# A new written-out order for all engines in sliding-window attention followed by an ELU feed-forward layer

## The chip, the cores and the metric

The kernel runs on one core of a Trainium2 chip. The metric is device time in microseconds (us); lower is better. A core has five engines that run side by side, each strictly in the order of its own instruction stream: TensorE (PE, matrix products), VectorE (DVE), ScalarE (ACT), GpSimd (POOL) and SyncE (SP, which here only issues DMA transfers). They wait for each other on semaphores. Matrix products land in PSUM, a small memory of eight banks, and have to be taken from there by DVE or ACT. TensorE's clock is granted by a throttle, and the profile shows which share of it was granted.

## The reference

There are 8 batches, 8 heads, 576 positions and a head size of 64. Attention is limited to a window of 32 positions to each side; its output, 4608 tokens of width 512, goes through two matrix products with an ELU between them.

```python
def _attn_ref(q, k, v):
    scores = (1.0 / np.sqrt(D)) * np.matmul(q, k.transpose(0, 1, 3, 2))
    mask = np.abs(pos[:, None] - pos[None, :]) <= 32
    scores = np.where(mask, scores, -1000000000.0)
    attn = np.exp(scores - np.max(scores, axis=-1, keepdims=True))
    attn = attn / (np.sum(attn, axis=-1, keepdims=True) + 1e-09)
    return np.matmul(attn, v)

def _moe_ref(x, w_in, w_out):          # x: 4608 x 512, w_in: 512 x 2048
    h = x @ w_in
    g = np.where(h > 0.0, h, np.exp(np.minimum(h, 0.0)) - 1.0)
    return g @ w_out                   # w_out: 2048 x 512

x = attn_out.transpose(0, 2, 1, 3).reshape(B * S, H * D)
```

## The kernel before

**Tiling.** The work unit is 64 query positions of one batch with all heads; there are 9 units in a batch and 72 in all. Two neighbouring units mostly form a group (`G`, line 409): groups 0 to 4 are batch 0, 5 to 8 batch 1. A group goes through these steps, and the name in brackets is the step's name in the plan: scores of all heads by 8 or 16 small products (QK, line 431), the exponential on ACT (SM, 444), the window mask on DVE (MK, 459), product with V in two halves of four heads (AV, 472), where a column of ones beside V gives the row sums, division by them on DVE (RN, 495 and 497), and a transpose of the result into `xt` (X). The transpose is a product with the identity on PE (513) and a copy for groups 0 to 8, and a transposing DMA on SP (509) from group 9 on.

Units are then gathered into token tiles of 2, 2, 2, 3, 4, 3 and then 8 units (`sizes`, line 597). For a tile the first product with w_in is done in pieces of up to 512 columns (H, line 537) into the three PSUM banks `psH`; ACT takes the exponential (EX, 546), ACT or DVE forms the clamped part (FF, 558 or 560), and DVE takes the maximum into `g_sb` (GG, 566 or 569), which frees the bank. `g_sb` holds 1024 tokens. Each chunk of 128 tokens is then multiplied with w_out in four parts of four products (Y, line 584), one for each quarter of w_out, all into one bank; ACT copies the result out (YC, 590) and issues the store (OUT, 594).

**Loads.** K, Q and V come as 32-bit blocks of 128 positions from SP (L, line 271; the blocks at the end are shorter). V blocks are cast into `vw` (CV, from line 345). From batch 2 on a K block and a Q block lie side by side in one buffer `sp`, are cast together on POOL (C2, line 311) and transposed by one DMA (XB, 324). For batch 0 the first half of the positions is loaded, cast (C), transposed on PE (T, 337) and copied (E). The second half of batch 0's K and Q and all of batch 1's come as 16-bit data by four and two DMAs from POOL (LR, line 363 on, issued at 383), are transposed on PE in small pieces (TR, 393) and copied (TTR). The weights too come from POOL, as four quarters each: `WI(c)` (655) and `WO(c)` (660). Quarter c of w_in serves the columns fo from 4c to 4c + 3; quarter c of w_out serves part c of each Y. All loads from POOL stand behind one wait (WAIT, 291) for batch 0's first Q block.

**What sets the order.** Nothing in the kernel is scheduled by a compiler. The class `Plan` (line 21) holds every step with its engine, an assumed duration, a rank and the steps that it depends on; it plays through a small model of the engines and of the DMA queues, and whenever an engine is free it takes the ready step with the lowest rank. The order that comes out is the order in which the instructions are issued; the chip then keeps each engine to it. `SHIFT` (618) moves single ranks, `ENG` (611) gives single steps to another engine, `DLAT` (33) is the assumed time from a transfer's end to its use, `RING` (643) how many transfers SP keeps outstanding, `LATE` an extra delay for two loads. The ranks of the loads of batch 0 start from the place in `FIRST` (721), those of POOL's queue from the place in `LINE` (723). Steps that hold a buffer (`psH`, `st`, `sp`, `cb`) are only taken when one is free in the model.

While the model has PE idle in the first 30 us (`WARM`), PE gets filler: products of the identity with itself into an unused corner of a PSUM bank (line 484). Their number comes from the idle time in the model:

```python
if start[n] < self.WARM:
    self.fill(max(0, int((start[n] - pe - 0.15) / 0.11)))
```

The dependency of a Y part on its quarter of w_out is written with an offset for chunk 0, so part 0 of chunk 0 names quarter 2, and its parts 1 to 3 name quarter 3; the product itself reads quarter `part`:

```python
deps.append(("WO", min(NWC - 1, part * YQ * NWC // NFO + 2 * (c == 0))))
```

Of the kernel before, what the change touches and what calls it, by code (L numbers as in the profile page):

```python
# [20 lines left out]
class Plan:  # L21
# [11 lines left out]
    DLAT = 1.9  # L33
# [22 lines left out]
    def run(self):  # L56
# [22 lines left out]
        def push(t, kind, x):  # L79
            heapq.heappush(events, (t, kind, next(seq), x))  # L80
# [23 lines left out]
        while len(order) < len(ops) or events or any(rings.values()):  # L104
# [4 lines left out]
            if nxt is not None and (te is None or now + nxt <= te):  # L109
                now += nxt  # L110
                for q in rings.values():
                    if q:
                        q[0][1] -= nxt / per
                        if q[0][1] <= 1e-9:
                            h = q.pop(0)
                            for a, k in self.acq.get(h[0], ()):
                                if a == "ring":
                                    held[a] += k
                                    for e in free:
                                        push(now, 1, e)  # L120
                            push(now + self.DLAT + self.late[h[0]], 0, h[0])
                continue
# [44 lines left out]
        for n in order:  # L167
            if ops[n][0] == "PE":
                if start[n] < self.WARM:
                    self.fill(max(0, int((start[n] - pe - 0.15) / 0.11)))  # L170
                pe = start[n] + ops[n][1]
            ops[n][4]()
# [3 lines left out]
def kernel(  # L176
# [423 lines left out]
    for t, n in enumerate(sizes):  # L600
# [11 lines left out]
        ("TT", 0, "k", 1): "DVE", ("CV", 0, 0, 1): "POOL", ("CV", 0, 2, 1): "DVE", ("CV", 0,  # L612
        2, 2): "ACT", ("C", 0, "q", 2): "POOL", ("TTR", 0, "k", 0): "ACT", ("TTR", 0, "k",
        1): "DVE", ("TTR", 0, "q", 1): "DVE", ("TTR", 1, "k", 1): "DVE", ("TTR", 1, "k", 2):
        "ACT", ("TTR", 1, "k", 3): "DVE", ("X", 5): "DVE", ("X", 6): "DVE", ("FF", 0, 8):
        "ACT", ("FF", 2, 8): "ACT", ("FF", 4, 0): "ACT", ("FF", 4, 2): "DVE", ("FF", 4, 8):
        "ACT", ("FF", 4, 14): "DVE", ("FF", 5, 8): "DVE", ("FF", 5, 14): "DVE"}
    SHIFT = {
        ("zvw", 2): 926, ("WI", 0): 54, ("WI", 1): 60, ("WI", 2): 47, ("WO", 0): 49, ("WO",
        1): 57, ("LR", 1, "k", 0): 107, ("LR", 1, "q", 0): 110, ("WO", 3): 61, ("L", 0, "k",  # L620
        0): 100, ("L", 0, "k", 1): 103, ("L", 0, "q", 0): 97.6, ("L", 0, "v", 0): 97, ("L",
        0, "v", 1): 30, ("L", 0, "k", 2): 100, ("L", 0, "q", 1): 35, ("L", 0, "v", 2): 85,
        ("L", 0, "q", 2): 99, ("C", 0, "q", 2): -1931, ("L", 0, "v", 3): 91, ("L", 1, "v",
        1): 219, ("GT", 2): 128, ("TT", 2, 0): 15, ("TT", 2, 2): 7, ("TT", 2, 4): 5, ("TT",
        3, 0): -10, ("TT", 3, 3): 9, ("TT", 3, 4): 2, ("TT", 4, 1): -9, ("TT", 4, 2): -5,
        ("TT", 4, 3): -31, ("TT", 4, 4): -40, ("TT", 5, 1): -102, ("TR", 0, "k", 1): -129,
        ("TR", 0, "q", 0): -179, ("TR", 1, "k", 0): -44, ("TR", 1, "q", 0): -16, ("TR", 1,
        "q", 1): -15, ("TR", 1, "q", 2): -40, ("TR", 1, "q", 3): -44, ("MK", 2): -1957,
        ("AV", 2, 1): -133, ("QK", 4): -168, ("RN", 4, 1): -2043, ("XT", 5): 64, ("QK", 6):
        -27, ("AV", 6, 0): 33, ("RN", 7, 0): -2117, ("XT", 7): 41, ("SM", 8): -2119, ("AV",  # L630
        8, 1): 42, ("AV", 9, 0): 98, ("X", 9): 19, ("RN", 10, 1): 85, ("X", 10): 16, ("QK",
        11): 58, ("X", 11): 14, ("X", 15): 8, ("X", 17): 2, ("QK", 19): -111, ("X", 19):
        -66, ("AV", 20, 1): -109, ("SM", 21): 43, ("AV", 21, 1): 21, ("RN", 21, 1): 21,
        ("H", 0, 0): -86, ("H", 0, 4): -191, ("GG", 0, 8): -2059, ("H", 1, 0): -59, ("H", 1,
        8): -181, ("H", 1, 12): -174, ("GG", 1, 12): -2063, ("H", 2, 4): -205, ("H", 2, 8):
        -187, ("H", 2, 12): -82, ("H", 3, 0): -75, ("H", 3, 4): -62, ("H", 3, 8): -217,
        ("FF", 3, 10): -2123, ("H", 3, 12): -29, ("H", 3, 14): 43, ("H", 4, 0): 26, ("H", 4,
        2): 45, ("H", 4, 6): -162, ("H", 4, 8): 44, ("H", 4, 10): -154, ("H", 4, 12): 69,
        ("H", 4, 14): -153, ("H", 5, 0): 49, ("H", 5, 2): 72, ("H", 5, 4): 96, ("GG", 5, 4):
        88, ("H", 5, 6): 73, ("H", 5, 8): 18, ("H", 5, 12): 91, ("H", 5, 14): 39, ("Y", 0,  # L640
        0): -95, ("Y", 0, 3): -64, ("Y", 1, 0): -66, ("Y", 1, 3): -58, ("Y", 2, 1): -45,
        ("Y", 2, 2): -41, ("Y", 2, 3): 36, ("Y", 4, 2): 72, ("Y", 11, 0): -126}
    RING, XBT = 2.2, 1.3
    LATE = {("L", 0, "v", 3): 1.0, ("L", 0, "v", 4): 1.0}
# [105 lines left out]
    for b in range(B):  # L750
        blocks = sorted(((group_of(b, nm, j), "kqv".index(nm), nm, j)
                         for nm in "kqv" for j in range(NTB)))
        for _, _, nm, j in blocks:
# [5 lines left out]
            if b:  # L759
                deps = [("GT", min(b, 2))]  # L760
                if deps[0] not in P.ops:
# [4 lines left out]
            pk = PK[nm][j] if b or nm == "v" or j < 2 else 16  # L766
            P.op(n, "SP", 0.62, rl, deps,
                 lambda b=b, nm=nm, j=j: L(b, nm, j, nc.sync),
                 dma=("S", pk, 16 if b else 15), late=LATE.get(n, 0.0),
                 acq=[("st", 1) if nm == "v" else ("sp", 0.5), ("ring", 1)])  # L770
# [31 lines left out]
            if nm == "k":  # L802
                continue
            r = min(r, prank(group_of(b, "k", j)))
            P.op(("C", b, j), "POOL", 1.25, r - CC, [("L", b, "k", j), n],
                 lambda b=b, j=j: C2(b, j, nc.gpsimd),
                 acq=("cb", 1), rel=("sp", 1))
            war = [("QK", qk(last(b - NKB)))] if b >= NKB else []
            P.op(("TT", b, j), "SP", XBT, r - XX, [("C", b, j)] + war,
                 lambda b=b, j=j: XB(b, j),  # L810
                 dma=("S", 64, 19), acq=("ring", 1), rel=("cb", 1))
    TRS = {b: [("TR", b, nm, part) for nm in "kq" for part in range(4 if b else 2)]
           for b in range(NBR)}
    for b in range(NBR):
        r = prank(gof[b * NQB if b else 4])
        for n in TRS[b]:
# [7 lines left out]
            P.op(m, eng, {"DVE": 0.72, "ACT": 0.64}[eng], r - 4, [n],  # L824
# [18 lines left out]
    for i in range(NG):  # L843
# [17 lines left out]
        if twin(i):  # L861
            P.op(("SM", i, 0), "ACT", 0.55, r - PER, deps, lambda i=i: SM(i, 0),
                 rel=("psT", 1))
            P.op(("SM", i), "ACT", 0.55, r - PER, [("SM", i, 0)],
                 lambda i=i: SM(i, 1), rel=("psH", 1))
        else:
            P.op(("SM", i), "ACT", 0.95, r, deps, lambda i=i: SM(i),
# [4 lines left out]
        P.op(("MK", i), "DVE", 0.7 if i < 5 else 1.0, r, deps, lambda i=i: MK(i))  # L872
        t, c = where[i]
        for g in range(2):
# [17 lines left out]
            P.op(("RN", i, g), "DVE", 0.58, r + 1 + g, deps,  # L892
# [12 lines left out]
        else:  # L905
            P.op(("X", i), "SP", 1.25, r + 3, deps, lambda i=i: X(i), dma=("S", 32, 19), acq=("ring", 0.5))

    hseq = [(t, fo) for t in range(NT) for fo in range(0, NFO, pack(t))]
    for n, (t, fo) in enumerate(hseq):
# [8 lines left out]
        if old >= 0:  # L918
            deps.append(("Y", old // 2, NFO // YQ - 1))
        P.op(("H", t, fo), "PE", 0.86 * fr, r, deps,  # L920
             lambda t=t, fo=fo: Hm(t, fo), acq=("psH", 1))
        deps = [("H", t, fo)]
        P.op(("EX", t, fo), "ACT", 0.09 + 0.43 * fr, r, deps,
# [3 lines left out]
             {"ACT": 0.2, "DVE": 0.1}[eng] + 0.4 * fr, r, [("EX", t, fo)],  # L927
# [4 lines left out]
        P.op(("GG", t, fo), "DVE", 0.12 + 0.52 * fr, r, deps,  # L932
             lambda t=t, fo=fo: GG(t, fo), rel=("psH", 1))
    NQ = NFO // YQ
    for c in range(NCH):
# [3 lines left out]
        for part in range(NQ):  # L939
# [9 lines left out]
            P.op(("Y", c, part), "PE", 0.86, r, deps,  # L949
# [5 lines left out]
        P.op(("YC", c), "ACT", 0.52, r, deps, lambda c=c: YC(c),  # L955
# [36 lines left out]
```

## Time and profile before

| | |
|---|---|
| median of 5 runs | 320.57 us (318.28 to 321.29) |
| the profiled execution | 320.57 us, span 318.8 us |
| PE busy | 305.5 us, 96% |
| PE weight loads | 172.0 us, 54% |
| DVE busy | 205.8 us, 65% |
| ACT busy | 210.1 us, 66% |
| POOL busy | 111.6 us, 35% |
| mean granted clock of TensorE | 0.984 |
| DMA | 51.43 MB in 153637 packets |

The span is the time from the first to the last recorded instruction of that one execution; its own device time is 1.8 us longer. In the profile a line such as "L537 PE MATMUL psH<-xt,w_in_sb" is a group of instructions: source line, engine, operation, output and inputs. Matmul ends are modelled and overlap, so a busy PE may still lose time between matmuls; how far their starts lie apart tells more. "12.40 0.40 PE ... [1.55 <-DVE cb L297]" is start, length, and how long the engine stood idle before it and what ended that. SPq and POOLq are the queues in which an engine issues DMAs.

### The profile page before, as it was taken

What the parts mean: (1) busy time and instruction counts of PE and PEld (TensorE: products, weight loads), DVE (VectorE), ACT (ScalarE), POOL (GpSimd) and SP (SyncE); (2) the same over time, 40 slices, a digit from 0 to 9 for tenths busy, and PEclk for the clock granted to TensorE, in tenths of its full rate; (3) what the DMA queues carried; (4) which work ended last, traced back from release to release, by engine and by line L of the source; (5) the groups of instructions that cost most, each with busy time, mean ns of one, the idle gap of its engine ahead of it and who ended that gap; (6) DMA issues with size and microseconds to landing.
All of it is one profiled execution on the core that took longest, in us unless ns stands there. A gap on an engine that the chain in (4) does not pass through costs nothing.

```text
span 318.8 us, 7692 instructions
## 1 busy us (share of the span) xinstructions
PE 305.5 (96%) x2974; PEld 172.0 (54%) x2974; DVE 205.8 (65%) x451; ACT 210.1 (66%) x357; POOL 111.6 (35%) x162
## 2 busy tenths in 40 slices
PE   7599999999999999999999999999999999999995
PEld 6488865686755444454444554445454545444442
DVE  5377776889965687784649667758474858444300
ACT  4237855767754988777877648777776776576711
POOL 4970046876443373334548342536000000000000
PEclk9958999999999999999999999999999999999999
DMA  8999996999999989999999989989411111100111
GB/s 187 208 202 206 205 197 167 249 207 226 205 209 184 250 156 208 183 219 192 218 242 253 190 206 179 243 188 216 86 52 49 51 49 51 49 33 33 63 73 66
DMA packets 153637, 51.43 MB, mean 161 GB/s; under 512 B 143104, under 2 KB 148992, under 8 KB 153600
## 3 DMA queue, kind: packets, MB, share of 16 engines
q1 hardware_dynamic: 142304, 35.53, 56.9%
q0 software_dynamic: 6112, 5.96, 11.5%
q10 hardware_dynamic: 5184, 9.44, 8.9%
q8 instruction: 23, 0.38, 0.5%
q14 instruction: 14, 0.11, 0.1%
HBM read 36.70 MB, written 9.44 MB: 145 GB/s over the span
## 4 chain that ended last, share of the span: by engine, by line
PE 73%; ACT 6%; DVE 6%; SPq 6%; DMA 5%; issue 2%; POOL 0%; ACTq 0%; DVEq 0%; POOLq 0%
PE psH L537 29%; PE psY L584 18%; PE psT L584 13%; PE psO L472 5%; SPq L271 4%; ACT e L546 3%; DMA sp<-in_k_dram 2%; ACT f L558 2%; PE psH L393 2%; PE psS L431 2%; DMA qk<-cb 2%; SPq L326 2%; DVE f L560 1%; DMA sp<-in_q_dram 1%; DVE g_sb L566 1%
## 5 line engine op out<-in xcount | busy, mean ns | idle before, releaser
L537 PE MATMUL psH<-xt,w_in_sb 128*128 128x512 bf16 (+3 forms) x832 | 147.5, 313 | 2.9 <-DVE g_sb L569 1.6
L546 ACT ACTIVATE e<-psH 128x512 f32<-128x512 f32 (+1 forms) x148 | 86.2, 584 | 62.8 <-PE psH L537 55.8
L566 DVE SCALAR_TENSOR_TENSOR g_sb<-f,psH 128x512 bf16<-128x512 bf16 (+1 forms) x106 | 70.7, 670 | 56.1 <-ACT f L558 49.7
L537 PEld LDWEIGHTS <-w_in_sb 128*128 128x128 bf16 x832 | 68.9, 98 | 52.1 <-issue 3.8
L584 PEld LDWEIGHTS <-g_sb 128*128 128x128 bf16 x576 | 53.4, 98 | 57.5
L297 POOL CAST vw<-st 64x512 bf16<-64x512 f32 (+2 forms) x105 | 67.4, 643 | 45.7 <-DMA st<-in_v_dram 38.3
L584 PE MATMUL psY<-w_out_sb,g_sb 128*128 128x512 bf16 x320 | 80.8, 379 | 0.0
L558 ACT ACTIVATE f<-e 128x512 bf16<-128x512 f32 (+1 forms) x106 | 65.7, 621 | 2.9
L584 PE MATMUL psT<-w_out_sb,g_sb 128*128 128x512 bf16 x224 | 56.8, 379 | 0.0
L297 POOL CAST cb<-sp 128x1024 bf16<-128x1024 f32 (+2 forms) x31 | 32.9, 1061 | 63.8 <-DMA sp<-in_q_dram 58.7
L459 DVE TENSOR_TENSOR pm<-pu,masks 128x512 bf16<-128x512 bf16 x72 | 35.1, 531 | 5.8 <-ACT pu L444 4.0
L472 PEld LDWEIGHTS <-pm 128*128 128x128 bf16 x576 | 26.9, 99 | 15.3 <-DVE xs L497 2.8
L497 DVE TENSOR_TENSOR xs<-psO,rc 128x256 bf16<-128x256 f32 (+1 forms) x71 | 30.1, 424 | 2.4
L444 ACT ACTIVATE pu<-psS 128x1024 bf16<-128x1024 f32 (+1 forms) x25 | 24.6, 983 | 10.6 <-PE psS L431 8.0
L569 DVE TENSOR_TENSOR g_sb<-psH,f 128x512 bf16<-128x512 f32 (+1 forms) x42 | 28.2, 671 | 3.0
L472 PE MATMUL psO<-vw,pm 128*128 128x65 bf16 x552 | 29.0, 195 | 0.6 <-DVE xs L497 0.2
L560 DVE TENSOR_SCALAR f<-e 128x512 bf16<-128x512 f32 (+1 forms) x42 | 22.6, 539 | 6.3 <-ACT e L546 6.1
L495 DVE RECIPROCAL rc<-psO 128x4 f32<-128x4 f32 (+1 forms) x71 | 12.5, 176 | 11.8 <-PE psO L472 11.0
L590 ACT COPY y<-psY 128x512 f32<-128x512 f32 x20 | 11.6, 578 | 7.2 <-PE psY L584 7.2
L431 PEld LDWEIGHTS <-qk 64*128 64x128 bf16 x576 | 10.3, 97 | 7.5 <-issue 6.9
L484 PE MATMUL psO<-ident 128*128 128x128 bf16 x114 | 10.9, 262 | 2.0 <-POOL ident masks.py:199 1.4
L431 PE MATMUL psS<-qk 64*128 64x64 bf16 x384 | 10.7, 197 | 0.0
(56 smaller groups left out, 113.2 us busy)
## 6 DMA issues: line engine op xcount, KB each, us to landing
out_dram<-y ACTq DMA_DIRECT2D x36, 256.0 KB, 2.6
sp<-in_q_dram SPq DMA_DIRECT2D x26, 256.0 KB, 4.1
sp<-in_k_dram SPq DMA_DIRECT2D x26, 256.0 KB, 4.0
st<-in_v_dram SPq DMA_DIRECT2D x24, 256.0 KB, 4.3
st<-in_v_dram SPq DMA_DIRECT2D x16, 192.0 KB, 4.6
w_in_sb<-in_moe_w_in_dram POOLq DMA_DIRECT2D x4, 512.0 KB, 12.4
w_out_sb<-in_moe_w_out_dram POOLq DMA_DIRECT2D x4, 512.0 KB, 16.8
sp<-in_k_dram SPq DMA_DIRECT2D x6, 128.0 KB, 3.7
```

Source lines behind the costliest of these rows:

```text
L297: eng.tensor_copy(dst, src)
L431: nc.tensor.matmul(ps[h % 2][:, s, hp, :], lhsT=kT[b % NKB][base:base + 64, hp, qb * QB:qb * QB + 128], rhs=qT[b % NKB][base:base + 64, hp ...
L459: nc.vector.tensor_mul(dst, pu[:, :, s], mb)
L472: nc.tensor.matmul(o[:, j, :], lhsT=p[:, h, s * QB:s * QB + 128], rhs=vw[b % NVB][:, qb, h, :], start=(s == 0), stop=(s == len(G[i]) - 1))
L497: nc.vector.tensor_mul(live["X", i][0:n, g * HP:(g + 1) * HP, :], o[0:n, :, 0:D], rb)
L537: nc.tensor.matmul(ps[:, f], lhsT=w_in_sb[:, do, (fo + f) * 128:(fo + f + 1) * 128], rhs=xts[t][:, do, :], start=(do == 0), stop=(do == ND ...
L546: nc.scalar.activation(e, ps, AX.Exp)
L558: nc.scalar.activation(f, e, AX.Relu, bias=1.0, scale=-1.0)
L560: nc.vector.tensor_scalar(f, e, -1.0, 0.0, ALU.add, ALU.min)
L566: nc.vector.scalar_tensor_tensor(g_sb[:, fo:fo + pack(t), gcols(t)], f, -1.0, ps, ALU.mult, ALU.max)
L569: nc.vector.tensor_tensor(g_sb[:, fo:fo + pack(t), gcols(t)], ps, f, ALU.max)
L584: nc.tensor.matmul(ps, lhsT=g_sb[:, fo, gc:gc + 128], rhs=w_out_sb[:, fo, :], start=(fo == 0), stop=(fo == NFO - 1))
```

## The change

All steps stay what they are and compute the same. What changes is the plan. The model gets a separate latency for each DMA queue and other durations for many steps; `SHIFT` and `ENG` are replaced as a whole; `LATE` is no longer used; `RING` goes from 2.2 to 2.8, and loads of batch 0 take a share of it by their size. Loads of a K and the Q block beside it, from batch 2 on, become one step that issues both DMAs one behind the other and takes a whole `sp` buffer; before they were two steps of half a buffer each. After 6.5 us of the model the number of filler products is worked out with 0.062 us for each instead of 0.11. The diff, cut to its core:

```diff
-    DLAT = 1.9
+    DLAT = {"S": 1.0, "A": 1.9, "P": 2.6}
...
-                            push(now + self.DLAT + self.late[h[0]], 0, h[0])
+                            push(now + self.DLAT[ops[h[0]][5][0]] + self.late[h[0]], 0, h[0])
...
-                    self.fill(max(0, int((start[n] - pe - 0.15) / 0.11)))
+                    self.fill(max(0, int((start[n] - pe - 0.1) / (
+                        0.11 if start[n] < 6.5 else 0.062))))
...
     SHIFT = {
-        ("zvw", 2): 926, ("WI", 0): 54, ("WI", 1): 60, ("WI", 2): 47, ("WO", 0): 49, ("WO",
-        1): 57, ("LR", 1, "k", 0): 107, ("LR", 1, "q", 0): 110, ("WO", 3): 61, ("L", 0, "k",
-        0): 100, ("L", 0, "k", 1): 103, ("L", 0, "q", 0): 97.6, ("L", 0, "v", 0): 97, ("L",
-        0, "v", 1): 30, ("L", 0, "k", 2): 100, ("L", 0, "q", 1): 35, ("L", 0, "v", 2): 85,
-        ("L", 0, "q", 2): 99, ("C", 0, "q", 2): -1931, ("L", 0, "v", 3): 91, ("L", 1, "v",
-        1): 219, ("GT", 2): 128, ("TT", 2, 0): 15, ("TT", 2, 2): 7, ("TT", 2, 4): 5, ("TT",
...
+        ("zvw", 2): 1067, ("WI", 1): -28, ("LR", 0, "k", 0): -38, ("LR", 0, "k", 1): -38.5,
+        ("LR", 0, "q", 0): -40, ("LR", 0, "q", 1): -40, ("WI", 3): -21, ("WO", 1): 44,
+        ("WO", 2): 30, ("LR", 1, "k", 0): -39, ("WO", 3): 34, ("L", 0, "k", 0): 13, ("L", 0,
+        "k", 1): 20, ("L", 0, "q", 0): 7, ("L", 0, "v", 0): 39, ("CV", 0, 1, 0): -1972,
+        ("CV", 0, 1, 1): -1990, ("CV", 0, 1, 2): -1988, ("L", 0, "q", 1): 16, ("CV", 0, 2,
+        0): -1992, ("CV", 0, 2, 1): -1980, ("L", 0, "v", 3): 134, ("L", 0, "v", 4): 4, ("L",
+        1, "v", 0): -57, ("L", 1, "v", 1): -55, ("L", 1, "v", 2): -63, ("L", 1, "v", 4):
+        -82, ("GT", 2): 176, ("C", 2, 0): 188, ("TT", 2, 0): -84, ("TT", 2, 1): -72, ("CV",
...
-    RING, XBT = 2.2, 1.3
-    LATE = {("L", 0, "v", 3): 1.0, ("L", 0, "v", 4): 1.0}
+    RING, XBT = 2.8, 1.33
...
+            if b and nm == "q":
+                continue
+            if b and nm == "k":
+                P.op(n, "SP", 1.27, rl, deps,
+                     lambda b=b, j=j: (L(b, "k", j, nc.sync), L(b, "q", j, nc.sync)),
+                     dma=("S", 2 * pk, 16.4), acq=[("sp", 1), ("ring", 1.5)])
+                P.op(("C", b, j), "POOL", 1.06, r - CC, [n],
...
-                 dma=("S", pk, 16 if b else 15), late=LATE.get(n, 0.0),
-                 acq=[("st", 1) if nm == "v" else ("sp", 0.5), ("ring", 1)])
+                 dma=("S", pk, 16.4),
+                 acq=[("st", 1) if nm == "v" else ("sp", 0.5), ("ring", 1 if b else pk / 64)])
...
-            P.op(("C", b, j), "POOL", 1.25, r - CC, [("L", b, "k", j), n],
...
-            P.op(m, eng, {"DVE": 0.72, "ACT": 0.64}[eng], r - 4, [n],
+            P.op(m, eng, {"DVE": 0.68, "ACT": 0.64}[eng], r - 4, [n],
...
-            P.op(("RN", i, g), "DVE", 0.58, r + 1 + g, deps,
+            P.op(("RN", i, g), "DVE", 0.55, r + 1 + g, deps,
...
-        P.op(("H", t, fo), "PE", 0.86 * fr, r, deps,
+        P.op(("H", t, fo), "PE", 0.863 * fr, r, deps,
...
-        P.op(("EX", t, fo), "ACT", 0.09 + 0.43 * fr, r, deps,
+        P.op(("EX", t, fo), "ACT", 0.07 + 0.43 * fr, r, deps,
...
-             {"ACT": 0.2, "DVE": 0.1}[eng] + 0.4 * fr, r, [("EX", t, fo)],
+             {"ACT": 0.14, "DVE": 0.08}[eng] + 0.4 * fr, r, [("EX", t, fo)],
...
-        P.op(("GG", t, fo), "DVE", 0.12 + 0.52 * fr, r, deps,
+        P.op(("GG", t, fo), "DVE", 0.11 + 0.5 * fr, r, deps,
```

The rest of the new `SHIFT` moves single QK, SM, AV, RN, X, H and Y steps, most of them in batches 0 to 2, and the new `ENG` moves single casts, copies and FF steps between DVE and ACT.

## The prediction

> **What bounds the kernel now.** I read the page's slices first, then the two-microsecond stages of the start, the order of time on PE, and the waits of PE after 30 us. Rows of engines and clock of the page:
>
> ```profile
> PE   7599999999999999999999999999999999999995
> PEclk9958999999999999999999999999999999999999
> DMA  8999996999999989999999989989411111100111
> ```
>
> PE is full from the fourth slice on (24 us). The clock row has one hole, in slices 3 and 4, and the DMA engines are full from the start to about 220 us. Stages (PE busy, its loads, DVE, ACT, POOL, granted clock, DMA share, GB/s):
>
> ```profile
> 12.00:14.00 2.00, 1.19 (x25) 0.85 (x25) 0.77 (x2) 0.35 (x1) 2.00 (x3) 1.00 1.20 178
> 14.00:16.00 2.00, 0.83 (x30) 0.80 (x32) 0.44 (x1) 0.94 (x2) 1.61 (x3) 0.86 1.27 197
> 16.00:18.00 2.00, 2.00 (x58) 1.72 (x56) 1.62 (x4) 0.64 (x1) 1.91 (x3) 0.50 1.24 198
> ...
> 24.00:26.00 2.00, 1.94 (x38) 1.49 (x37) 1.12 (x4) 1.09 (x2) 0.00 (x0) 0.58 1.24 205
> 26.00:28.00 2.00, 2.00 (x52) 1.85 (x49) 1.54 (x6) 1.40 (x3) 0.00 (x0) 1.00 1.24 206
> ```
>
> After a stretch in which PE worked about half of the time, the clock is at half from 15.45 to 25.69 us (10.24 us), most of which PE is full. PE in order of time (start, length, what, idle before):
>
> ```profile
> 9.35 1.50 PE L484 MATMUL psO<-ident 128*128 128x128 bf16 x24
> 12.40 0.40 PE L337 MATMUL psH<-ident,cb 128*128 128x128 bf16 x4 [1.55 <-DVE cb L297]
> ...
> 15.36 1.44 PE L393 MATMUL psH<-ident,g_sb 48*64 48x48 bf16 x48
> ...
> 20.33 0.60 PE L472 MATMUL psO<-vw,pm 128*128 128x65 bf16 x8
> ...
> 26.02 1.06 PE L537 MATMUL psH<-xt,w_in_sb 128*128 128x128 bf16 x16
> ```
>
> L484 is filler. 24 of them last 1.50 us, some 0.056 us each, though the planner counted 0.11: they cover half of the gap they were put into. The first product with w_in starts at 26.02. Later waits of PE:
>
> ```profile
> PE psH L537 <- DVE g_sb L569: 1.6, 4, 0.5
> PE psH L537 <- DVE g_sb L566: 0.7, 2, 0.5
> ```
>
> After 30 us almost nothing is left to remove. From the starts of all matmuls, gaps over 0.15 us beyond the streaming time come to 5.0 us in 13 places between 30 and 123 us, none later. So PE is the bound from 26 us, the end is 3.9 us after the last matmul's start at 314.9, and what can be won is a start before 26 us plus at most 5 us.
>
> **What the Trainium skill says.** "TensorE: Matmul & The Clock Gate", Part 1: the clock is set from activity in windows of about 3.4 us, half rate when PE was idle; a 128-column matmul costs 107 ns cold, 56 ns warm. The trace agrees: the cold stretch is three such windows and fillers are 0.107 us apart before 5.2 us, 0.056 after. It puts the drop after an idle window; here PE was half busy, so how much filler holds the clock is not known. "DMA: Bandwidth & Descriptors", Queues, rings and completion order (Arbitration): the engines alternate between the queues that have work. The trace agrees: the 32-row k load issued at 8.29 beside POOL's loads landed at 14.65, 6.36 us, where 128-row loads alone took about 4.
>
> **The change part by part.** Landing times are those of each issue in the trace.
>
> *Filler.* After 6.5 us a gap gets its length over 0.062 instead of 0.11, 1.77 times as many. A warm gap of 2.8 us gets (2.8 - 0.1) / 0.062 = 43 fillers of 0.056, 2.4 us of work, not 24 and 1.34. In the cold stretch the spacings of useful matmuls sum to some 6 us (filler left out, 2.7 us), half of which is the half clock: 3.0 us at most. Bounds: nothing (the clock falls anyway) to 3.0. If cold, 43 fillers take 4.6 us in a 2.8 us gap and delay what stands behind them by 1.8. I take warm.
>
> *Order of the first loads on SP.* Ranks with the new shifts give v1, k2, v2, q2, q0, k0, v4, k1, q1, v0, v3; before it was v4, v1, q1, v2, q0, k0, v0, v3, k1, k2, q2. q0, which lets POOL start, stands behind 2.5 instead of 3.75 loads of 128 rows; landings of full loads are 1.0 us apart (4.62, 5.52, 6.81, 7.72, 8.61), so 6.5 instead of 7.7. The 32-row k2 and q2, which landed at 14.65 and 16.04 and held the transposes at 15.17 and 17.27 and all behind them on the in-order PE, come some 10 us sooner. v0, needed by the first AV, is now last but one; shared with POOL's queue it lands at about 15, against 9.9, still before the AV that stood at 20.33.
>
> *POOL's queue.* Before: four pieces of batch 0 (landed by 16.2), then w_in 3 at 18.7, w_out 2 at 21.4, w_in 2, 0 at 24.2, 26.7, w_out 0 at 29.3, w_in 1 at 32.6, w_out 1, 3 at 35.2, 37.8, k and q of batch 1 at 41.3, 45.0. New ranks: the four pieces, batch 1's k, w_in 1, 3, 0, 2, w_out 0, batch 1's q, w_out 2, 3, 1. The engines were full, so bytes set the times: k of batch 1 costs 3.5 (41.3 - 37.8), a weight 2.6. First w_in: 18.7 + 3.5 = 22.2; all four by 22.2 + 3 x 2.6 = 30.0 instead of 32.6. Then w_out 0 at 32.6, q at 36.3; v of batch 1 comes in between (five loads, 4.6 us at 1.0 a full load), so w_out 2, 3, 1 at about 43, 46, 49.
>
> *First H.* The first group's x was ready at 25.5. The chain to it began with k2's cast at 14.67 and ran through cold PE work; 3.0 less for the clock, and several us less for k2, q2, put it before 22. So w_in decides: 26.0 - 22.2 = 3.8 us gained. Worth 0 if x stays at 25.5, at most 5 if w_in lands sooner.
>
> *Does the head start survive?* Until 49 us PE lives mostly without Y. There are 12 blocks of H of 0.93 us and 8 of 0.66 (batch 0, 16.5 us), 3 us of the remaining attention of batch 0, 3.4 of L393 transposes for batch 1, 4.4 of its attention, 7 of tile 4: 34 us against 27. ACT and DVE (8.3 and 8.1 of 10 us busy at 30 to 40) have to keep up: an H block costs them about 0.6 + 0.69 + 0.55 = 1.85, 0.93 each, equal to PE. It survives, except for one wait. Y(0, 1) multiplies by w_out 1, but its entry in the plan names w_out 3, which now lands one weight sooner. PE is in order; behind Y(0, 1) stand the H blocks, for which ACT and DVE wait once three psH banks are drained. Bounds 0 to 2.6 us, half: +1.3.
>
> *New order from 60 us on, durations, DVE/ACT swaps.* Not seen anywhere; between losing as much as there is to win and winning it all, +5 to -5. The largest waits stand where DVE's g_sb was late (73, 80 to 83, 108, 122 us), and the new durations are near the trace (filler apart: RN 0.55 for 0.17 + 0.42, cast of a block 1.06 for 1.061, TTR on DVE 0.68, 0.76 in the trace). I take -1.5.
>
> *k and q in one SP step.* The same two DMAs, 1.27 us of SP. Hidden: POOL's cast waits 58.7 us in all for q, and works some 110 of 319 us; K and V stand three batches deep. Uncovered it would cost the longest such wait, 4.8 us, once. Nothing. Removed LATE, DLAT, RING only shift the plan: nothing of their own.
>
> Sum: 318.8 - 3.8 + 1.3 - 1.5 = 314.8 of span; the profiled execution took 1.8 more than its span and equals the median of the five, 320.57: **316.6 us**.
>
> **Rivals.** *The clock falls all the same:* filler follows planned gaps, and 1.55 us before 12.40 was an unplanned one. Then the 3.8 shrink to about 1.5: 318.9. *The head start is handed back at w_out:* less work is in reach than I count, since batch 1's attention goes through ACT and DVE in series, and PE idles 3.8 us more between 38 and 49: 320.4. For it: the DMA engines are full, and all of it landed by 49.8 before. Against: 34 us of work. *Slower:* at Y(0, 1) PE stands waiting for w_out 1, planned at 42 or earlier while it lands at 49. From 3.8 + 1.5 us of stall the gain is gone; with 6 us the 1.3 becomes 6 (319.5 + 1.8 = 321.3), and as that is an idle stretch longer than the one before 15.45, the clock falls for 10.24 us, which with PE full costs 5.1: 326.4. Against: that stall needs the plan's landing to be wrong by two weights.
>
> **How the numbers follow.** Chances: forecast 0.59 (its own range 311.5 to 318.9: all of the 5 us won, or the stall in full and nothing won), clock falls 0.10 (318.9, half faster, half no change), handed back 0.10, slower 0.21. No change is within 0.5%, what a measurement of this kernel can tell: 319.0 to 322.2. Faster 0.64, same 0.15, slower 0.21. The range 310.5 to 324.5 leaves out the deep end of the slower case and a sliver below.
>
> **What would show it.** Right: granted clock 1.00 from about 5 to the end, first L537 near 22, w_in 1 landed first, L472 before 19, and the last matmul's start near 311. Wrong: a hole in the clock row; PE waiting at L584 between 40 and 50 us with w_out just landing; gaps on g_sb after 60 us over 5 us in sum. If x and not w_in is late at the first L537, the step on the loads failed.

## The result, and the profile after

The changed kernel takes **320.25 us** (median; 318.35 to 323.13) against 320.72 us of the kernel before on the same chips: ratio **0.9996**, 95% interval 0.9982 to 1.0010. Nothing that can be measured came of it; forecast were 316.6 us and 0.64 for faster. The profiled execution took 322.63 us with a span of 320.6, so it is 2.4 us over its own median; f2's below, 322.01 us, is 2.5 over its own, and one kernel's executions spread over some 318 to 324 us. Times of places are read below from such single executions, verdicts from the intervals. Lines of the changed file are one higher than before (L537 is now L538, L484 is L485). Table entries without a profile row are counted from the trace's single instructions.

The page's slices of the changed kernel, first rows of part 2:

```profile
PE   6987999999999999999999999999999999999995
PEclk9999999999999999999999999999999999999999
DMA  7999989999799989998999999996111211100021
```

The hole in the clock row is gone, as forecast. But there is a new dent, 7, in PE's fourth slice (24 to 32 us), where the kernel before had a 9. The two-microsecond stages (PE busy, its loads, DVE, ACT, POOL, granted clock, DMA share, GB/s):

```profile
14.00:16.00 2.00, 2.00 (x68) 1.74 (x67) 1.39 (x4) 1.93 (x4) 1.96 (x3) 1.00 1.28 207
16.00:18.00 2.00, 1.32 (x46) 1.08 (x40) 1.52 (x5) 1.15 (x2) 1.33 (x3) 1.00 1.21 207
...
24.00:26.00 2.00, 1.51 (x50) 1.22 (x42) 1.54 (x6) 1.97 (x3) 0.00 (x0) 1.00 1.24 206
26.00:28.00 2.00, 1.05 (x19) 0.94 (x17) 0.99 (x3) 0.00 (x0) 0.00 (x0) 1.00 1.24 208
```

At full clock PE is busy 1.05 of 2 us at 26 to 28, where it was full before; ACT and POOL are idle there too. PE in order of time (start, length, what, idle before):

```profile
16.72 0.41 PE L473 MATMUL psO<-vw,pm 128*128 128x65 bf16 x8
16.97 0.41 PE L473 MATMUL psY<-vw,pm 128*128 128x65 bf16 x8
17.87 0.66 PE L485 MATMUL psO<-ident 128*128 128x128 bf16 x9 [0.49 <-DVE xs L498]
...
25.83 0.38 PE L485 MATMUL psO<-ident 128*128 128x128 bf16 x4 [0.49 <-DVE xs L498]
26.05 1.00 PE L538 MATMUL psH<-xt,w_in_sb 128*128 128x128 bf16 x15
28.42 0.22 PE L538 MATMUL psH<-xt,w_in_sb 128*128 128x128 bf16 x1 [1.37 <-issue]
28.48 0.39 PE L514 MATMUL psT<-ident,xs 128*128 128x128 bf16 x4
```

Two things stand out. Filler (L485) *waits*: it is written into a corner of the same buffer, psO, as the result of the AV products, so behind an AV it stands until DVE has read that buffer (L498). And PE stops after 15 of the 16 products of an H block: the sixteenth waits for no semaphore, its releaser is "issue". The first H, which the forecast put at 22.2 us, starts at 26.05, as before (26.02), though its first quarter of w_in landed at 22.69 and the first group's x was ready at 20.57. Waits of PE after 30 us:

```profile
PE psO L473 <- DVE xs L498: 1.8, 4, 0.7
PE psH L538 <- DVE g_sb L567: 1.3, 4, 0.6
```

These are 3.1 us, where before showed 2.3 for g_sb; the forecast had 1.5 less.

### The profile page after: what moved, and what is told of

Same layout as the page of the kernel before. It is cut to its first block, busy times and chain, and to the rows that moved or that the text cites. A ratio compares the mean times of both kernels' runs of the same rounds, so it can differ in the third digit from the quotient of the medians.

```text
span 320.6 us, 7783 instructions
## 1 busy us (share of the span) xinstructions
PE 306.6 (96%) x3013; PEld 171.6 (54%) x3013; DVE 207.5 (65%) x443; ACT 215.4 (67%) x365; POOL 111.0 (35%) x162
## 3 DMA queue, kind: packets, MB, share of 16 engines
q0 software_dynamic: 6112, 5.96, 11.3%
## 4 chain that ended last, share of the span: by engine, by line
PE 73%; DVE 10%; ACT 5%; DMA 5%; issue 3%; SPq 2%; POOL 0%; DVEq 0%; POOLq 0%
PE psH L538 32%; PE psY L585 15%; PE psT L585 14%; PE psO L473 5%; DVE pm L460 4%; DMA sp<-in_q_dram 4%; DVE xs L498 2%; SPq L272 2%; DVE g_sb L567 2%; PE psS L432 2%; ACT e L547 1%; PE psH L394 1%; ACT pu L445 1%; PE psO L485 1%; DMA qk<-cb 1%
## 5 line engine op out<-in xcount | busy, mean ns | idle before, releaser
L538 PE MATMUL psH<-xt,w_in_sb 128*128 128x512 bf16 (+3 forms) x832 | 147.5, 314 | 2.9 <-issue 1.4
L567 DVE SCALAR_TENSOR_TENSOR g_sb<-f,psH 128x512 bf16<-128x512 bf16 (+1 forms) x111 | 74.4, 671 | 58.3 <-ACT f L559 54.6
L538 PEld LDWEIGHTS <-w_in_sb 128*128 128x128 bf16 x832 | 68.8, 98 | 49.6 <-issue 1.8
L298 POOL CAST vw<-st 64x512 bf16<-64x512 f32 (+3 forms) x106 | 67.9, 641 | 51.0 <-DMA st<-in_v_dram 42.2
L559 ACT ACTIVATE f<-e 128x512 bf16<-128x512 f32 (+1 forms) x111 | 68.9, 621 | 3.3
L298 POOL CAST cb<-sp 128x1024 bf16<-128x1024 f32 (+1 forms) x30 | 31.9, 1064 | 52.6 <-DMA sp<-in_q_dram 50.5
L460 DVE TENSOR_TENSOR pm<-pu,masks 128x512 bf16<-128x512 bf16 x72 | 41.2, 614 | 5.7 <-ACT pu L445 2.7
L473 PEld LDWEIGHTS <-pm 128*128 128x128 bf16 x576 | 24.8, 97 | 18.4 <-DVE xs L498 7.4
L498 DVE TENSOR_TENSOR xs<-psO,rc 128x256 bf16<-128x256 f32 (+1 forms) x71 | 30.1, 424 | 2.4
L570 DVE TENSOR_TENSOR g_sb<-psH,f 128x512 bf16<-128x512 f32 (+1 forms) x37 | 24.9, 672 | 3.0
L561 DVE TENSOR_SCALAR f<-e 128x512 bf16<-128x512 f32 (+1 forms) x37 | 19.6, 531 | 4.5 <-ACT e L547 4.2
L485 PE MATMUL psO<-ident 128*128 128x128 bf16 x153 | 14.1, 253 | 2.9 <-DVE xs L498 1.5
L485 PEld LDWEIGHTS <-ident 128*128 128x128 bf16 x153 | 11.7, 115 | 2.9 <-POOL ident masks.py:199 1.4
```

The source lines that it names most:

```text
L298: eng.tensor_copy(dst, src)
L460: nc.vector.tensor_mul(dst, pu[:, :, s], mb)
L473: nc.tensor.matmul(o[:, j, :], lhsT=p[:, h, s * QB:s * QB + 128], rhs=vw[b % NVB][:, qb, h, :], start=(s == 0), stop=(s == len(G[i]) - 1))
L485: nc.tensor.matmul(live["W"][:, 384:512], lhsT=ident, rhs=ident, start=True, stop=True)
L498: nc.vector.tensor_mul(live["X", i][0:n, g * HP:(g + 1) * HP, :], o[0:n, :, 0:D], rb)
L538: nc.tensor.matmul(ps[:, f], lhsT=w_in_sb[:, do, (fo + f) * 128:(fo + f + 1) * 128], rhs=xts[t][:, do, :], start=(do == 0), stop=(do == ND ...
```

## The experiments

Three questions: is the time lost to the filler, to the clock, or to what comes after the head start? The expectations stand as they were written before each run. Ratios are to the kernel before, with 95% intervals.

### The filler rule on both orders

Only the filler rule was exchanged, the new one put into the kernel before and the old one into the changed kernel.

```diff
# f1_before_new_fill
-                    self.fill(max(0, int((start[n] - pe - 0.15) / 0.11)))
+                    self.fill(max(0, int((start[n] - pe - 0.1) / (
+                        0.11 if start[n] < 6.5 else 0.062))))
# f2_after_old_fill: the same in reverse
```

> The kernel before with nothing but the new filler rule. Theory A (the start counts: PE's lead at 24 us reaches the end unless something takes it): no half clock, first L537 near 24 instead of 26, 1 to 2 us faster, 318.5 to 319.5. Theory B (the start does not count: what PE does between 26 and 48 us is set by ACT, DVE and the loads, so PE's clock before 26 us is slack): granted clock full, time within 0.5 us of before, 320.2 to 321.2.

> The kernel after with the old filler rule alone (0.11 us for each filler, everywhere). Theory A: the clock falls to half for about 10 us in the start and the lead of 1.9 us is gone, 1 to 2 us slower than the kernel after, unless the clock holds without the filler; the stall of PE at 26.8 us goes or moves, which gives 1.4 back. Theory B: within 0.5 us of the kernel after.

f1 took 321.39 us, **1.0052** [1.0029, 1.0076]; f2 319.51 us, **0.9983** [0.9960, 1.0007]. More filler on the old order makes it slower, although the clock was at half only from 22.49 to 25.90 us instead of 15.45 to 25.69. In f2 the clock fell later than before, at 23.33, though its interval does not set it apart from the change. PE in order of time in f2:

```profile
21.20 0.23 PE L431 MATMUL psS<-qk 64*128 64x64 bf16 x4
24.09 0.50 PE L431 MATMUL psS<-qk 64*128 64x64 bf16 x12 [2.66 <-issue]
```

Again PE stops inside a block of products, for 2.66 us, without a wait. The same in f1: 1.56 us, ending at 20.57 us.

The filler might be too many instructions, so the next kernel covers the same time with half as many, each 252 columns wide:

```diff
# f3_after_wide_fill
-        for _ in range(n):
-            nc.tensor.matmul(live["W"][:, 384:512], lhsT=ident, rhs=ident,
+        wide = _bap(ident, [ident.ap[0], [0, 2], [1, 126]])
+        for _ in range((n + 1) // 2):
+            nc.tensor.matmul(live["W"][:, 260:512], lhsT=ident, rhs=wide,
```

> The kernel after with half as many fillers of 252 columns instead of 128: the same PE time in half the instructions. Tells what the stall of 1.53 us at 26.84 us is, in the middle of a block of L538 that waits for no semaphore. If PE ran out of fetched instructions there (a 16 KB block of the instruction queue starts at 26.10 and ends at 27.07), the fetches come later and the stall is gone, clock still full; under theory A the kernel is then about 1.4 us faster than after, 318.5 to 319.5, under theory B the same time. If the stall is something else, it stays at the same place.

322.16 us, **1.0107** [1.0064, 1.0150]: slower than the change itself. Half as many filler instructions did not help.

### Does a later first H cost its time, and do ACT and DVE set the pace behind it?

Eighteen wide fillers (1.9 us) ahead of the first H delay everything behind it. In g2 the ELU of batch 0 is left out (a plain copy takes its place), so that ACT and DVE have less to do there.

```diff
# g1_after_late_start, in the function that issues H, once
+        while late[0]:
+            late[0] -= 1
+            nc.tensor.matmul(live["W"][:, 260:512], lhsT=ident, rhs=wide,
+                             start=True, stop=True)
# g2_after_light_h, in EX and in FF
+        if t < 4:
+            return
# and in GG
+        if t < 4:
+            nc.vector.tensor_copy(g_sb[:, fo:fo + pack(t), gcols(t)], es.pop((t, fo)))
+            return
```

> The kernel after with 18 filler products of 252 columns (18 x 0.107 = 1.9 us of PE) put right before the first L538. Nothing else changes. Theory A (the start counts): 1.9 us slower than the kernel after, about 322.2. Theory B (PE's place before 26 us is slack, since ACT, DVE and the loads set the pace up to about 60 us): under 0.6 us slower; PE's lag of 1.9 us at 28 us is gone from the trace by 60 us.

> The kernel after with the ELU of batch 0 (token tiles 0 to 3) left out: no exponential and no clamped part there, DVE copies h. This takes 0.6 + 0.6 us from ACT or DVE for each of 20 blocks between 26 and 50 us and leaves PE, loads and order alone. Theory B: PE gets its banks back sooner, useful work done by 45 us rises by 1.5 us or more and the kernel is 1 us or more faster. If the written order and w_out's arrival hold PE there and not ACT and DVE: under 0.6 us.

g1: 321.39 us, **1.0072** [1.0046, 1.0099], 0.76% or 2.4 us over the change, for 1.9 us of added filler. In useful work (the measure is explained in the part on the prediction) it lags 1.3 us behind the change at 30 us and still 1.0 at 60. So most of the delay is not absorbed there. g2: 319.44 us, **1.0007** [0.9986, 1.0027]: nothing gained that can be measured, so ACT and DVE are not what costs the changed kernel its time in batch 0.

### No filler behind 6.5 us

```diff
# g3_after_no_late_fill (g4_before_no_late_fill: the kernel before, with its 0.15)
-                    self.fill(max(0, int((start[n] - pe - 0.1) / (
-                        0.11 if start[n] < 6.5 else 0.062))))
+                    if start[n] < 6.5:
+                        self.fill(max(0, int((start[n] - pe - 0.1) / 0.11)))
# g5_after_no_fill: pass, no filler at all
```

> The kernel after with no filler at all behind 6.5 us of the plan. Theory A: the clock is at half for 10 us or more before 30 us, 2 to 3 us slower than the kernel after. Theory B: the clock falls too, but the time stays within 0.6 us of 320.25; with fewer instructions PE does not run out of fetched ones, so no stall over 1 us without a semaphore.

> The kernel before with no filler behind 6.5 us of its plan. The theory now: late filler costs more than the clock it holds; PE in its fixed order stands behind it, and with it runs out of fetched instructions. Then this kernel is faster than before, by 0.3 to 1.0%, though PE is at half clock up to about 20 us; and as the new order without late filler was at 0.9934, the rest up to there is what the new order is worth. Rival: the new order needs less clock, its first loads come earlier, and in the old order the missing filler costs 1 us or more: 1.003 or slower.

> The kernel after with no filler at all; against the kernel without the late filler alone (0.9934) 23 more products go, at 1.4 to 4 us, where PE has nothing to do anyway. Theory: within 0.3% of that, 0.990 to 0.997. If filler is worth something as long as it stands in nothing's way, it is slower, 0.998 or more.

The old rule's plan has PE's first step behind 6.5 us, so g4 has no filler left at all; g3 keeps 23, before 3.8 us, and g5 shows that these matter little. These are the fastest kernels of the case. g3: **317.42 us, 0.9934** [0.9914, 0.9953]; g4: 318.21 us, **0.9940** [0.9918, 0.9962]; g5: 318.05 us, **0.9935** [0.9907, 0.9963]. g3 beats both the kernel before and the change. PE in g3 in order of time:

```profile
13.59 1.48 PE L394 MATMUL psH<-ident,g_sb 48*64 48x48 bf16 x48
15.00 0.62 PE L473 MATMUL psO<-vw,pm 128*128 128x65 bf16 x8
...
22.19 0.41 PE L473 MATMUL psO<-vw,pm 128*128 128x65 bf16 x8
22.44 0.41 PE L473 MATMUL psY<-vw,pm 128*128 128x65 bf16 x8
22.68 1.05 PE L538 MATMUL psH<-xt,w_in_sb 128*128 128x128 bf16 x16
25.05 0.40 PE L514 MATMUL psT<-ident,xs 128*128 128x128 bf16 x4 [1.31 <-DVE pm L460]
```

And in g4:

```profile
14.34 1.48 PE L394 MATMUL psH<-ident,g_sb 48*64 48x48 bf16 x48
18.27 0.62 PE L473 MATMUL psO<-vw,pm 128*128 128x65 bf16 x8
...
22.92 1.90 PE L538 MATMUL psH<-xt,w_in_sb 128*128 128x128 bf16 x16
```

Forty-eight transposes in 1.48 us instead of 0.94: PE runs at half rate, in g3 until 21.09 us and in g4 until 26.59. The first H comes at 22.68 and 22.92 all the same, 3.4 and 3.1 us sooner than with filler. In g3 the forecast of 22.2, set by w_in, is nearly met, without the warm clock that was to make it possible. And g4, the *old* order at half clock, gets there at almost the same time: it was the filler and not the clock that held the first H of the kernel before at 26.02.

### Which filler, and why

Four kernels, all made from the change, divide the filler. h1 makes each filler behind the first gap 16 columns instead of 128. x1 keeps filler only up to 15 us of the plan, x2 only before 6.5 and from 15 us on, and x3 is x1 with the wide filler of f3.

```diff
# h1_after_thin_fill
+        w = 16 if calls else 128
+        calls.append(n)
-            nc.tensor.matmul(live["W"][:, 384:512], lhsT=ident, rhs=ident,
+            nc.tensor.matmul(live["W"][:, 384:384 + w], lhsT=ident, rhs=ident[:, 0:w],
# x1_after_fill_to_15 (x3_after_wide_fill_to_15: and f3's edit)
-                if start[n] < self.WARM:
+                if start[n] < 15.0:
# x2_after_fill_from_15
+                if start[n] < 6.5 or 15.0 <= start[n] < self.WARM:
```

> The kernel after with as many fillers as it has, those behind the first gap with 16 columns instead of 128: the same instructions in less than half of the PE time. If what filler costs is PE's time in front of useful work, the time goes most of the way to the kernel without late filler, 0.995 or less. If it is the fetch of instructions, PE runs out of them as before or sooner, with a stall of 1 us or more without a semaphore between 15 and 30 us, and the time stays at 0.998 or more.

> The kernel after with its filler up to 15 us of the plan and none behind (about 101 of the 130 late ones, in gaps in which PE mostly waits for loads). Theory T, filler costs PE's time in front of useful work: these stand where there is little useful work, so the time is near the kernel without late filler, 0.993 to 0.996. Theory I, filler uses up fetched instructions: these 101 products with their loads are 202 instructions, four fifths of a 16 KB block, so PE still runs out between 16 and 28 us, with a stall without a semaphore of 0.6 us or more in sum, and the time is 0.997 or more.

> The kernel after with its filler between 6.5 and 15 us of the plan left out and that behind kept (about 29 products, 1.6 us warm, 3.1 us at half clock, between the steps of batch 0's attention). Theory T: these stand in front of useful work, 0.997 or more. Theory I: few instructions, no stall, 0.993 to 0.996.

> As the kernel after with filler up to 15 us of the plan alone, with half as many fillers of 252 columns. That one was at 0.9985, with stalls of 1.06, 1.44 and 0.45 us without a semaphore. If those are PE waiting for fetched instructions, and they are what keeps it from the 0.9934 of no late filler, about 51 products with their loads less bring the sum of such stalls under 1.5 us and the time to 0.996 or less; if the clock is then full before 20 us, a warm start may even give 0.990. If the stalls do not depend on the number of instructions, 0.998 or more.

Between 14 and 31 us (waits and stops from start to start, so somewhat longer than the idle time that the profile gives; the filler's busy time from its group):

| kernel | median us | ratio | filler's waits for DVE | filler busy | stops without a wait |
|---|---|---|---|---|---|
| change | 320.25 | 0.9996 [0.9982, 1.0010] | 2.05 | 3.9 (x47) | 2.34 |
| h1, thin | 319.46 | 0.9988 [0.9966, 1.0011] | 1.75 | 2.4 (x41) | 0 |
| x1, to 15 us | 319.41 | 0.9985 [0.9964, 1.0006] | 0 | 1.6 (x22) | 2.94 |
| x3, to 15 us, wide | 320.70 | 1.0015 [0.9996, 1.0033] | 0 | 1.5 (x11) | 3.03 |
| x2, from 15 us | 321.49 | 1.0070 [1.0044, 1.0095] | 1.75 | 3.6 (x27) | 0 |
| g3, none | 317.42 | 0.9934 [0.9914, 0.9953] | 0 | 0 | 1.53 (put down to DVE in the waits; see below) |

**Late filler stands in the way.** x2 differs from g3 only in filler from 15 us on and is 1.36% (4.3 us) slower. PE of x2 in order of time:

```profile
17.27 1.12 PE L485 MATMUL psO<-ident 128*128 128x128 bf16 x9 [0.29 <-DVE xs L498]
...
22.77 1.14 PE L485 MATMUL psO<-ident 128*128 128x128 bf16 x9
...
28.17 0.38 PE L485 MATMUL psO<-ident 128*128 128x128 bf16 x4 [0.49 <-DVE xs L498]
28.39 1.06 PE L538 MATMUL psH<-xt,w_in_sb 128*128 128x128 bf16 x16
```

At half clock nine fillers take 1.12 us, and each batch of them behind an AV waits for DVE first. The waits are 1.75 us and the fillers, by the spacing of their starts, 2.92, together 4.67 us, and the first H starts 5.7 us later than in g3. Behind it g3 loses 1.53 us in a stop that x2 does not have, which leaves 4.2: the size of the loss. h1 shortens the fillers but leaves the waits, and gains nothing measurable over the change. It fits neither of its two expectations: no stop, and no gain. That its clock was at half until 25.06 us may offset what it saved; no run separates this.

**A warm PE runs out of instructions.** x1 has no filler from 15 us of the plan on, and yet loses 0.5% to g3. PE of x1 in order of time:

```profile
17.35 0.24 PE L394 MATMUL psH<-ident,g_sb 48*64 48x48 bf16 x5 [0.87 <-issue]
...
23.59 1.04 PE L394 MATMUL psH<-ident,vw 64*64 64x64 bf16 x36 [1.25 <-issue]
...
29.51 0.66 PE L538 MATMUL psH<-xt,w_in_sb 128*128 128x128 bf16 x9 [0.23 <-issue]
```

The profile page's table of DMA queues has a queue for instructions:

```profile
q8 instruction: 23, 0.38, 0.5%
```

23 transfers, 16 KB each; PE's 6026 matmuls and weight loads come to some 260 for each, so I take them for PE's program coming in. Set beside PE's stops, from the trace's list of transfers; the last column counts PE's recorded matmuls and weight loads from the start up to the stop:

```
kernel  fetch (us)       PE stops at  goes on at   after the fetch's end   counted
change  14.04 to 15.03   16.16        16.54        1.51                    447
change  20.25 to 21.18   22.12        22.50        1.32                    701
change  26.10 to 27.08   26.84        28.42        1.34                    957
f1      18.30 to 19.27   18.82        20.57        1.30                    703
f2      21.78 to 22.76   21.24        24.09        1.33                    701
f3      17.14 to 18.07   18.58        19.52        1.45                    446
g3      22.80 to 23.74   23.52        25.05        1.31                    702
g5      24.28 to 25.23   25.93        26.57        1.34                    702
x1      14.99 to 15.93   16.29        17.35        1.42                    447
x1      21.14 to 22.07   22.15        23.59        1.52                    701
x1      27.24 to 28.21   29.07        29.51        1.30                    957
x3      16.86 to 17.81   17.59        19.24        1.43                    446
x3      22.98 to 23.92   23.88        25.26        1.34                    701
```

Thirteen times PE goes on 1.30 to 1.52 us after the end of a fetch, and every time it has stopped at one of three counts: 446 or 447, 701 to 703, 957. These are some 255 instructions apart, as many as the mean above gives for one transfer, and quite different work stands there: transposes, scores, AV products, H. So a stop belongs to a place in PE's stream and not to a product or a rank. The stop of g3 is put down to DVE's mask product in the waits, but the transposes need DVE's xs, done at 23.83 us, 1.2 us before they start; it is at 702 and belongs here.

Nine more stops at these counts, three each in g1 and g2, two in f5 (below) and a second one in f3, end 1.22 to 1.39 us after their fetch. In none of the 17 traces does PE pass such a place sooner than that. Kernels without a stop come to it later by themselves: h1, at half clock until 25.06 us, passes the three places 1.5 us or more after the fetch's end, the kernel before 2.9 us or more.

So PE waits there for its next block of instructions, and in this stretch the blocks set a pace. From one place to the next the change took 5.96 and 5.92 us (16.54, 22.50, 28.42), x1 6.24 and 5.92, and g3 5.93 (19.12 to 25.05) though it began at half clock. Filler takes up places in the blocks as useful products do: x1 has 101 fillers more than g3, with their weight loads 202 instructions, by estimate 4.7 us at 5.94 us for 255, and its first H, with no filler behind 15.5 us, starts at 26.60, 3.9 us later than in g3. x3, with half the filler, stops as long as x1 (3.03 us against 2.94): it has 0.7 us more useful work done by 24 us but still comes to the same counts too soon. Why it is no faster than x1 in the end is open. No run here delivers the instructions faster; what shows the fetch as the cause is this agreement in place and time, not an edit.

### Two further suspects

The mask product on DVE is longer in the changed kernel while POOL casts beside it. Its group, before and then after:

```profile
L459 DVE TENSOR_TENSOR pm<-pu,masks 128x512 bf16<-128x512 bf16 x72 | 35.1, 531 | 5.8 <-ACT pu L444 4.0 <-ACT pu L447 1.7
```

```profile
L460 DVE TENSOR_TENSOR pm<-pu,masks 128x512 bf16<-128x512 bf16 x72 | 41.2, 614 | 5.7 <-ACT pu L445 2.7 <-ACT pu L448 2.3 <-PE psO L473 0.6
```

Both kernels were run without POOL's casts of V in batches 3 to 7 (f5 the change, f6 the kernel before; that work is left out):

```diff
# in the cast of V blocks
+        if b >= 3:
+            return
```

> The kernel after without the casts of V on POOL for batches 3 to 7 (the attention of these batches then multiplies by older V; all else is unchanged, the order too). Tells what POOL's casts cost DVE's mask product L460, which takes 0.39 us alone and 0.81 in the mean with a POOL cast beside it. If that is the loss of 2.3 us between 140 and 240 us, the mask product falls to about 0.4 to 0.5 there, PE's waits on DVE at L473 go, and the time falls by 1.5 to 2.5 us against the kernel after. If not, under 0.5 us.

> The kernel before without the casts of V on POOL for batches 3 to 7 (their attention multiplies by older V), beside the same edit of the kernel after, which took 319.01 us against 320.25. If POOL's casts cost the new order more than the old one, and this is what it lost after 140 us, the kernel before gains clearly less than 1.2 us by the edit, 319.7 to 320.2. If both orders pay the same for the shared casts, it gains as much, 318.7 to 319.3, and the new order's loss lies elsewhere.

f5: 319.01 us, 0.9975 [0.9943, 1.0006]; f6: 318.92 us, 0.9988 [0.9968, 1.0009]. The group's mean falls to 514 and 516 ns, so the slowing by POOL is real, 614 to 514 ns in the change (0.42 us alone and 0.81 beside a cast there, by the trace). PE's waits for DVE from 140 us on, 1.7 us in the profiled change, are gone in f5. But both intervals take in 1, and the two ratios do not differ measurably: whatever it costs in time is below what these runs resolve.

Last, w_in ahead of batch 1's k in POOL's queue, on g3:

```diff
# h2_after_w_in_first
-        ("LR", 1, "k", 0): -39,
+        ("LR", 1, "k", 0): 0,
```

> The kernel after without late filler (0.9934) and with batch 1's k moved behind the four quarters of w_in and w_out's first in POOL's queue (one rank of the plan, which is worked out anew). Tests the step that w_in's landing sets the first L538: w_in 1 should land near 18.5 instead of 21.8, and x of the first group is there at 18.0. If it does, the first L538 comes 2 us or more sooner and, as PE's lead has reached the end so far, the kernel is 1 to 2 us faster, 0.987 to 0.990. If the lead is handed back because batch 1's k is late and w_out and ACT and DVE set the pace at 36 to 45 us, it stays at 0.992 or more.

332.71 us, **1.0373** [1.0320, 1.0427], and inconclusive as to its worth: w_in did land from 19.8 us on and the first H started at 20.91, 1.8 us sooner than in g3, as it should if w_in's landing sets it there; but one rank moved the whole plan. Its waits of PE:

```profile
PE psO L473 <- DVE xs L498: 5.7, 6, 1.4
...
PE psS L432 <- DMA qk<-cb: 2.4, 1, 2.4
```

PE waits 2.4 us near 100 us for a transposing DMA of a later batch. That the other shifts fit only the plan that they were tuned with is my reading, not shown.

## Why the prediction was wrong

The orders and filler rules as a table (ratio to the kernel before):

| filler behind 6.5 us | old order | new order |
|---|---|---|
| none | 0.9940 (g4, no filler at all) | 0.9934 (g3; 0.9935 for g5, no filler at all) |
| one for each 0.11 us | 1 | 0.9983 (f2) |
| one for each 0.062 us | 1.0052 (f1) | 0.9996 (change) |

Each column gets worse with more filler; only the last step of the new order, 0.9983 to 0.9996, is not clear of the noise. From the left to the right the order alone is worth 0.06%, 0.17% and 0.56%, of which only the last is clear of it. The forecast of the order and filler together was 4.0 us, 1.25%.

And the useful work that PE has done by a time (each weight load counted with the streaming time that a product of its width takes at full clock, filler left out, us):

| at us | before | change | g4 (old order, no filler) | g3 (new order, no filler) |
|---|---|---|---|---|
| 24 | 4.65 | 6.51 | 6.20 | 8.21 |
| 30 | 9.31 | 9.66 | 10.66 | 12.70 |
| 36 | 14.30 | 15.05 | 16.00 | 18.02 |
| 45 | 22.88 | 22.35 | 24.74 | 25.19 |
| 60 | 36.98 | 35.92 | 38.47 | 39.08 |
| 240 | 210.78 | 209.05 | 213.15 | 213.80 |

- **The filler step failed, and with it the 3.8 us of the first H.** The first H came at 26.05 us against 26.02 before, so 0 was won there. The mechanism of the clock held: it stayed at full from 9.30 us on, and "I take warm" was right. The price was wrong: warm filler was counted as free where it stands in a gap of the plan, and the half clock at up to 3.0 us. g4 shows the reverse. At half clock until 26.59 us the old order without filler has done 1.55 us more by 24 us than the kernel before, and starts H 3.1 us sooner. From 14 to 31 us filler cost the kernel before 2.43 us of its own, by the spacing of starts, and 0.60 of waits, 3.03 in all; the change 3.05 and 2.05. Nor did the sum have a term for PE's stops, 2.34 us in that stretch of the change. The bound "nothing to 3.0" left out a loss (a delay was named for a cold PE alone), though the profile before showed filler waiting for DVE's xs:

```profile
22.44 0.80 PE L484 MATMUL psO<-ident 128*128 128x128 bf16 x6 [0.53 <-DVE xs L497]
```

- **Landings held.** q0 landed at 6.82 (forecast 6.5), the first w_in at 22.69 (22.2), the last of the four at 30.35 (30.0). The last of w_out landed at 43.83 rather than 49, because the v of batch 1, which was put between them, was issued only from 38.2 us.
- **"So w_in decides" failed.** In the change w_in and x were both there by 22.69, but PE was still at fillers, transposes and attention in front of the first H. In g3 the time was met within 0.5 us, 0.85 us after the landing.
- **The head start.** By 24 us the change is 1.86 us ahead of the kernel before. It loses 1.5 of that by 30 us, with the 1.58 us stop inside the H block lying right there, is 0.5 behind at 45 and 1.1 behind at 60. f5 and f6, which have the same starts, show it again: 1.4 ahead at 24, 0.9 behind at 45 and 1.3 at 60. Without filler the new order is 2.0 ahead at 36 and 0.45 at 45. So part of the rival "handed back" came true too, in its own place. It named PE idling at w_out; in g3 Y(0, 1) waits 0.46 us for w_out 1 at 44.01 and an H block 0.82 us for g_sb at 38.94, while in the change no product waits for w_out. ACT's load over 30 to 39 us, g3 and then g4:

```profile
30.00:39.00 9.00, 8.21 (x149) 7.50 (x147) 7.56 (x18) 8.78 (x17) 0.00 (x0) 1.00 1.23 206
```

```profile
30.00:39.00 9.00, 8.64 (x140) 7.83 (x139) 6.56 (x15) 7.43 (x15) 0.00 (x0) 1.00 1.23 204
```

- ACT is busy 8.78 of 9 us in the new order and 7.43 in the old: there was hardly room for it to keep up, as the step "Does the head start survive?" said that it would. That this takes the 1.6 us back is argued; g2, which lightened both engines in the change and gained nothing, speaks against it being so there.
- **The wait at Y(0, 1), +1.3:** none in the change. **New order from 60 us on, -1.5:** between 60 and 240 us the change does 173.13 us of useful work and the kernel before 173.80, so it is +0.7 by these two executions. But the eleven traces with the new order and no work left out from 60 us on lie between 173.1 and 176.7, the three with the old one between 173.7 and 174.6: neither the size nor the sign is known. **k and q in one step, nothing:** POOL's waits for Q went from 58.7 to 50.5 us, and no wait of PE shows it.
- **The rival with the clock** did not occur in the change. The slower rival did not either.
- **Slips of the working, without effect on the outcome.** The row of PE has its first 9 in the third slice, so PE was 90% busy or more from 16 us on and not from 24. By its own terms the forecast's range is 311.8 to 319.4 us rather than 311.5 to 318.9.

Left open: an edit that delivers the instructions sooner, and what in the new order between 36 and 45 us loses what it won.

## What to carry to other kernels

Filler that keeps a clock up is work like any other: it has to be shown that it ends before the next useful instruction could start, also when the plan's gap does not open, and it must not be written into a buffer that another engine still reads. Before a faster clock is given a price, take the filler out and run it; here the cold start without filler was the fastest of all, on both orders. And a gap inside a run of equal products, with no semaphore behind it, should be held against the instruction queue's transfers and against the count of the engine's instructions: if it stands at the same count in kernels that differ, it is no product's fault.

## What the runs showed that was not expected

- PE stopped for 0.25 to 2.85 us without a wait that explains it, 22 times in 11 kernels, always at one of three counts of its instructions some 255 apart, and went on 1.22 to 1.52 us after a 16 KB fetch that itself took 0.9 to 1.1 us while the DMA engines were full.
- The granted clock is no measure of a cold start: in g4 it reads 1.00 throughout, while 48 transposes at 14.34 us took 1.48 us, as at half clock. The row showed only the later drop from full to half. The Trainium skill ("TensorE: Matmul & The Clock Gate", Part 1) tells of cold and warm durations; here those, and not the clock row, say which it is.
- Sixteen-column filler did not warm PE: h1 was at half clock until 25.06 us, the change only until 9.30.
